# Batch 0's keys ahead of its values, and fences by halves, in a retention layer fused with a swish feed-forward

## Chip, cores and metric

The kernel runs on one core of one Trainium2 chip. The metric is the device time of one launch in microseconds (us). The kernel before took 292.37 us in the median of 3 runs (291.78 to 292.76).

An engine's short name is used throughout: PE is the matmul engine (PEld its weight loads), DVE the vector engine, ACT the scalar engine, POOL the engine that the code calls gpsimd, SP the engine whose queue issues nearly all DMAs (SPq in the profile).

## What is computed

A retention layer (attention with a decay instead of a softmax) for 8 batches, 8 heads, 576 positions and heads of 64, then a feed-forward layer with 2048 hidden units and the activation h * sigmoid(beta * h):

```python
scores = scale * np.matmul(q, k.transpose(0, 1, 3, 2))
gamma = 1.0 - 2.0 ** (-5.0 - np.arange(H))
Dmat = np.where(rel >= 0, gamma[:, None, None] ** rel[None, :, :], 0.0)   # rel = row - column
attn = np.matmul(scores * Dmat, v)
x = attn.transpose(0, 2, 1, 3).reshape(B * S, H * D)                      # 4608 x 512
h = x @ w_in                                                              # 512 x 2048
out = (h * (1.0 / (1.0 + np.exp(-beta * h)))) @ w_out                     # 2048 x 512
```

Inputs and output are float32; the matmuls run in bfloat16.

## The kernel before

**Tiling.** Each batch has 512 positions in four chunks of 128 (a pair of batch and chunk has one number, `i`; batch 0 has chunks 0 to 3) and a tail of 64; the eight tails make up a ninth block of 512 rows. The decay is put into q and v ahead of time (`gq`, `gv`), so that a causal mask is all that is left for the scores inside a chunk; what earlier chunks give comes through a running state, the 64 x 64 sum of k times v for each head. The output of a chunk is therefore masked scores times values (`a_O`, `outputs4`) plus queries times the state of all earlier chunks, the cross part (`a_cross`, `crosses4`).

**Batch 0** opens the kernel, with nothing beside it but loads and a few warm-up matmuls on zeros (`warm_up`, L259). For chunk `i`: `pre` (L324) casts the keys to bf16 on POOL (L354) and multiplies the values by their gain on POOL (L328); `t_k` transposes the keys on PE (L384) and copies them out on ACT (L385); `a_sc` makes the scores (L403, two PSUM banks, tag "sc" with 2 buffers, or "mm" for chunk 3) and DVE masks them (`R`, L407, two instructions); `a_st` (L464) adds this chunk to the state in PSUM (L472) and copies it as bf16 to `sbds[c]` (L478, two instructions of half the rows each on ACT); `a_cross` multiplies queries by `sbds[c - 1]` (L436); `a_O` multiplies masked scores by values (L450); `a_x` copies the output to `xT` (L459, L460, L462), the input of the up projection.

The order is written out by hand in the body of the kernel (from L856): all calls are recorded in that order, and each engine runs its own in that order. In PE's queue, batch 0's steps stand like this (sc scores, st state, x cross, O output, a number for the chunk): tk0 sc0 st0, tk1 O0 sc1 x1, tk2 st1 O1 sc2, tk3 sc3 x2 st2 O2, x3 O3, up projection with st3 in front of it.

**Loads.** SP issues q of batch 0, then keys and values in the order `ahead` (L108; a pair is chunk and 0 for keys or 1 for values), then the first weights in pieces (L185): three column pieces of 256, each as two halves of the rows, a fourth of 256 whole, then pieces of 512 columns by row halves. `cast_w_in` (L201) casts a piece to bf16: even row blocks on POOL (L206), odd ones on DVE (L208).

**The up projection of batch 0** follows the pieces: `ups` (L797) makes two or four column blocks of 128 for a half `u` of the rows, and then again for the other half; `up` makes one column block in one go (L714). `fill` (L910) is the list of these steps and, behind them, of all other up and down projections; `streams` holds all other work with a place in `fill`, to fractions of a step, at which `merged` puts it in.

**Batches 2 to 7** do all four chunks at once (`scores`, `outputs4`, `crosses4`, for the tails `tail_outputs`, `tail_crosses`). Here each matmul uses a quarter of the array: 64 rows (a half of the positions or one head of a pair) and 64 columns. A cross matmul (`cross`, L612) reads the rows `row_d(j)` and writes the output rows `row_d(j ^ y)`; `paired` deals the lists of `j = 0` and `j = 1` alternately onto PE. The outputs of half `x` are written by the row half `x` of the array; a cross with `j == x` may follow at once, one with `j != x` has to wait until the outputs in the same PSUM bank are done. For that there is `fence` (L504): a tiny ACT copy (L505) that waits for the last output matmul, and for which the first cross of the second kind on row half 0 waits. `crosses4` puts the state matmuls of the next batch between the two kinds (`ahead`) for batches 3 to 6. `both4` is outputs and crosses of one batch, put into `fill` at a place such as `t + 25.9`.

Of the kernel before, what the change touches and what calls it, by code (L numbers as in the profile page):

```python
# [14 lines left out]
ALU = mybir.AluOpType  # L15
# [4 lines left out]
def kernel(  # L20
# [86 lines left out]

    ahead = [(0, 0), (0, 1), (1, 0), (1, 1), (2, 0), (3, 0), (2, 1), (3, 1)]  # L108
    keys_first = [(0, 0), (1, 0), (0, 1), (1, 1), (2, 0), (3, 0), (2, 1), (3, 1)]
# [74 lines left out]
    low_rows, high_rows = slice(0, KO // 2), slice(KO // 2, KO)  # L184
    pieces = [(f, 256, (low_rows, high_rows) if f < 768 else (slice(0, KO),)) for f in range(0, d_ff // 2, 256)]  # L185
    pieces += [(f, 512, (w,)) for f in range(d_ff // 2, d_ff, 512) for w in (low_rows, high_rows)]
# [83 lines left out]
    def betas_safe():  # L270

        nc.gpsimd.tensor_tensor(tiny[:], beta_sb[:], beta_sb[:], ALU.mult)
        nc.gpsimd.tensor_scalar(tiny[:], tiny[:], 1e-24, 1e-12, ALU.is_lt, ALU.mult)
        nc.gpsimd.tensor_tensor(beta_sb[:], beta_sb[:], tiny[:], ALU.add)

# [20 lines left out]
    def gains(g, c):  # L296
        return g[:, c, :].unsqueeze(2).to_broadcast([P, H, D])
# [26 lines left out]
    def pre(i, js=(0, 1)):  # L324

        b, c = seq[i]
        if 0 not in js:
            nc.gpsimd.tensor_tensor(live[i]["vn"][:], kv_tiles.pop(i)[:, 1], gains(gv, row_of(b, c)), ALU.mult)  # L328
            return
# [134 lines left out]
    def a_st(i):  # L464

        b, c = seq[i]
        L = live[i]
        if c == 0:
            state_ps[b] = psum.tile([P, HP, P], F32, name="st", tag="st", bufs=1)
        st = state_ps[b]  # L470
        for p in range(HP):
            nc.tensor.matmul(st[:, p, :], heads(L["kn"], p), heads(L["vn"], p),  # L472
                             start=(c == 0 and p == 0), stop=True, skip_group_check=True)
        for j in range(2):
            r, cols = slice(j * D, (j + 1) * D), slice(j * D, (j + 1) * D)
            e = nc.vector.tensor_copy if i in (CB + 2, CB + 3) else nc.scalar.copy
            if c < CB - 1:
                e(sbds[c][r, :, cols], st[r, :, cols])  # L478
                continue
            e(ends[b][r, :2], st[r, :2, cols])  # L480
            e(ends[b][(1 - j) * D:(2 - j) * D, 2:], st[r, 2:, cols])
# [4 lines left out]
    def row_d(j):  # L486
        return slice(j * D, (j + 1) * D)
# [101 lines left out]
    def outputs4(b):  # L589

        i0 = b * CB
        O4, opened = new_O4(i0, [P, 2, CB, 2 * PC]), set()
        R = batch[b]["R"]
# [8 lines left out]
        for y in range(2):  # L602
            paired(*[[F(one, x, y, cc, pp, kind, hh ^ x) for cc in range(2) for pp in range(2) for kind in range(2)
                      for hh in range(2)] for x in range(2)])
        batch[b]["O4"] = O4, fence()

    def crosses4(b, later=None):
# [4 lines left out]
        def cross(j, e, y, pp, after):  # L612
            p, c, kind = 2 * y + pp, e // 2, e % 2
            w = c // 2 * PC + kind * PC // 2
            mm(O4[c % 2, y][row_d(j ^ y), pp, :, w:w + PC // 2], sbq[e - 1][row_d(j), p, :],
               q_cols(i0 + c, row_d(j), p, kind)[0], after=after)

        def crosses(j, x, after=None):
            return [F(cross, j, e, y, pp, after) for e in range(1, 2 * CB) if e // 2 % 2 == x for pp in range(2) for y in range(2)]

# [45 lines left out]
    def tail_outputs(i0):  # L666

        O4, opened, R = new_O4(i0, [P, 2, NT, TL]), set(), live[i0]["R"]

# [6 lines left out]
        for y in range(2):  # L676
            paired(*[[F(one, x, y, t, pp, hh ^ x) for t in range(NT) for pp in range(2) for hh in range(2)]
                     for x in range(2)])
        live[i0]["O4"] = O4, fence()

    def tail_crosses(i0, later):
# [3 lines left out]
        def cross(j, x, t, y, pp, after):  # L685
            p = 2 * y + pp
            mm(O4[x, y][row_d(j ^ y), pp, t, :], ends[2 * t + x][row_d(j), p, :], live[i0 + t]["qkT"][row_d(j), 0, p, half(x)],
               after=after)

        for own in range(2):  # L690
            paired(*[[F(cross, j, j ^ own, t, y, pp, after if own else None) for t in range(NT) for pp in range(2) for y in range(2)]
                     for j in range(2)])
# [164 lines left out]
    betas()  # L857
    betas_safe()
    for n in range(4):
        pre_q(0, n)  # L860
    t_q(0, 0)
    warm_up(1, 128)
    t_q(0, 1)
    pre(0)
    t_k(0)
    warm_up(2, 128)
    a_sc(0)
    a_st(0)
    pre(1)
    t_k(1)  # L870
# [4 lines left out]
    a_sc(1)  # L875
    a_cross(1, True)
    pre(2, (0,))
    t_k(2)
    a_st(1)
    a_O(1)  # L880
    pre(3, (0,))
    a_sc(2)
    t_k(3)
    a_x(1)
    warm_up(1, 128)
    a_sc(3)
    a_cross(2, True)
    pre(2, (1,))
    a_st(2)
    a_O(2)  # L890
    a_x(2)
    pre(3, (1,))
    warm_up(2, 128)
    a_cross(3, True)
    a_O(3)
    cast_w_in(0, (0, 1))
    a_x(3)
# [11 lines left out]

    fill = [F(ups, 0, (fo, fo + 1), u, tags) for fo, tags in ((0, ("mm", "mm")), (2, ("O", "O")), (4, ("sc", "sc"))) for u in range(2)]  # L910
    fill += [F(up, 0, fo) for fo in (6, 7)]
    for fo, tags in ((8, ("O", "O", "sc", "sc")), (12, ("mm", "mm", "mm", "st"))):
# [110 lines left out]
    for n in range(1, B):  # L1023
# [17 lines left out]
        elif n < SB:  # L1041
            streams.append([(t + 16, F(first_states, b))] * (b == XB + 1) +
                           [(t + 19, F(group1, b, (0, 1))), (t + 25.9, F(both4, b))])
        elif n == B - 1:
# [41 lines left out]
```

## Time and profile before

One execution was profiled: 292.13 us, of which its span (first to last instruction) is 290.4 us. PE's granted clock is 1.00 in every stage up to 270 us.

| engine | busy us | share of span | instructions |
|---|---|---|---|
| PE | 280.4 | 97% | 3357 |
| PEld | 171.3 | 59% | 3385 |
| ACT | 172.6 | 59% | 306 |
| DVE | 168.4 | 58% | 314 |
| POOL | 119.6 | 41% | 219 |

By stage, PE is busy for 14.95 us of the first 18 (with overlapping matmuls and warm-ups counted), 5.66 of the 6 up to 24 us, 8.95 of the 9 up to 33 us and 26.89 of the 27 up to 60 us. Batch 0's keys and values land from 7.4 to 15.8 us at about 220 GB/s, in the order of their issue, some 1.2 us apart: k0 7.43, v0 8.64, k1 9.9, v1 11.1 (both from when POOL takes them up), k2 12.25, k3 13.46, v2 14.66, v3 15.80. The halves of the first weight pieces follow at 16.56 and 17.35, and the fourth piece at 23.30.

The seven fences ran at 79.93, 109.14, 140.10, 161.06, 188.05, 217.03 and 245.34 us.

A timeline row is read like this: start in us, length in us, engine, line, operation, output<-inputs, shapes, how many are merged into the row, and in square brackets the idle time of the engine before it and what ended it. For a merged row the length runs from the first start to the last end. The chain of waits has start, length and what the time went to.

### The profile page before, as it was taken

To read this page: it belongs to the slowest core of one execution; us is meant where nothing else is said; L and a number is where in the kernel's file an instruction comes from. 1 tells how busy PE (TensorE), PEld (TensorE's weight loads), DVE (VectorE), ACT (ScalarE), POOL (GpSimd) and SP (SyncE) were. 2 spreads that over 40 slices of the span, in tenths; PEclk is the share of its full clock that TensorE was granted. 3 is DMA by queue.
4 is the path that set the end of the run, shared out by engine and by line. 5 is a ranking of instruction groups with operands and counts; after the bars stand their busy time and mean duration, and the time that the engine had idled before them with its cause. 6 is when DMAs were issued, how large, how long until landed. Compare 5 with 4: busy or idle time off the path is not lost.

```text
span 290.4 us, 8109 instructions
## 1 busy us (share of the span) xinstructions
PE 280.4 (97%) x3357; PEld 171.3 (59%) x3385; DVE 168.4 (58%) x314; ACT 172.6 (59%) x306; POOL 119.6 (41%) x219
## 2 busy tenths in 40 slices
PE   8899999999999999999999999999999999999995
PEld 6554446864544454445554885578557845784584
DVE  6563556804673375405538976986597555642673
ACT  4676646686639895882257725772576156837730
POOL 4765206782565473337349245615389000000000
PEclk9999999999999999999999999999999999999999
DMA  7999999999999999599999979996789130003004
GB/s 211 218 341 386 387 275 227 253 187 194 214 153 258 251 277 189 139 254 175 193 257 217 170 113 257 260 162 142 234 192 169 41 148 3 2 29 116 2 2 142
DMA packets 128884, 54.01 MB, mean 186 GB/s; under 512 B 110400, under 2 KB 121680, under 8 KB 128848
## 3 DMA queue, kind: packets, MB, share of 16 engines
q1 hardware_dynamic: 128816, 53.49, 82.9%
q8 instruction: 26, 0.43, 0.7%
q14 instruction: 10, 0.08, 0.1%
q10 hardware_dynamic: 32, 0.01, 0.0%
HBM read 36.71 MB, written 9.44 MB: 159 GB/s over the span
## 4 chain that ended last, share of the span: by engine, by line
PE 86%; SPq 6%; DMA 4%; issue 1%; DVE 1%; POOL 1%; ACT 0%; DVEq 0%; POOLq 0%
PE ph L714 39%; PE po L824 16%; PE U L751 9%; PE Z L751 6%; PE W L751 6%; SPq L100 3%; PE O L499 3%; DMA wt<-in_moe_w_in_dram 3%; PE ph L806 2%; DMA kvn<-in_k_dram 2%; PE sc L499 1%; PE st L499 1%; SPq L198 1%; PE sc L403 0%; DVE sum L535 0%
## 5 line engine op out<-in xcount | busy, mean ns | idle before, releaser
L714 PE MATMUL ph<-xT,w_in_sb 128*128 128x512 bf16 (+1 forms) x544 | 113.9, 363 | 1.4 <-issue 0.6
L721 ACT ACTIVATE gT<-ph,beta_sb 128x512 bf16<-128x512 f32 (+1 forms) x100 | 63.6, 644 | 42.1 <-PE ph L714 41.2
L714 PEld LDWEIGHTS <-w_in_sb 128*128 128x128 bf16 x560 | 53.5, 98 | 55.7 <-POOL w_in_sb L206 0.9
L824 PE MATMUL po<-w_out_sb,gT 128*128 128x512 bf16 x246 | 56.2, 379 | 1.2 <-issue 1.0
L354 POOL CAST kn<-kvn 128x128 bf16<-128x128 f32 (+2 forms) x80 | 30.2, 411 | 58.1 <-DMA kvn<-in_k_dram 57.7
L751 PEld LDWEIGHTS <-sa 128*128 128x128 bf16 x400 | 39.2, 98 | 4.5
L719 DVE TENSOR_SCALAR gT<-hs,ratio 128x512 bf16<-128x512 f32 x40 | 23.8, 594 | 29.1 <-ACT hs L718 28.9
L824 PEld LDWEIGHTS <-gT 128*128 128x128 bf16 x256 | 24.2, 98 | 27.8
L317 POOL TENSOR_TENSOR qs<-qn,gq 128x256 bf16<-128x256 f32 (+1 forms) x36 | 27.5, 792 | 23.3 <-DMA qn<-in_q_dram 14.8
L328 POOL TENSOR_TENSOR vn<-kvn,gv 128x512 bf16<-128x512 f32 x32 | 34.4, 1079 | 4.9 <-DMA kvn<-in_v_dram 4.4
L718 ACT ACTIVATE hs<-ph,beta_sb 128x512 f32<-128x512 f32 x40 | 27.5, 687 | 14.4 <-PE ph L714 13.8
L735 DVE TENSOR_TENSOR sa<-gT 128x1024 bf16<-128x1024 bf16 (+1 forms) x45 | 33.9, 792 | 1.1 <-PE Z L751 0.9
L286 DVE TENSOR_TENSOR R<-sc,late 128x512 bf16<-128x512 f32 x24 | 15.3, 680 | 22.3 <-PE sc L499 12.1
L751 PE MATMUL Z<-b,sa 128*128 128x256 bf16 x160 | 19.1, 273 | 0.0
L751 PE MATMUL U<-b,sa 128*128 128x256 bf16 x160 | 19.1, 273 | 0.0
L248 DVE TENSOR_TENSOR b<-wt 128x512 bf16<-128x512 f32 x20 | 13.8, 736 | 7.1 <-ACT b L244 7.1
L751 PEld LDWEIGHTS <-gT 128*128 128x128 bf16 x160 | 15.6, 98 | 2.9
L407 DVE TENSOR_TENSOR R<-sc,causal 128x512 bf16<-128x512 f32 x16 | 10.2, 686 | 4.6 <-PE sc L403 4.5
L806 PE MATMUL ph<-xT,w_in_sb 128*128 128x512 bf16 x54 | 12.3, 379 | 0.3 <-ACT xT L460 0.2
L809 ACT ACTIVATE gT<-ph,beta_sb 128x512 bf16<-128x512 f32 x14 | 8.6, 686 | 4.2 <-PE ph L806 4.2
L831 ACT COPY ot<-po 128x512 f32<-128x512 f32 x12 | 7.0, 583 | 6.8 <-PE po L824 6.7
L629 ACT CAST xT<-O 128x512 bf16<-128x512 f32 x17 | 8.8, 597 | 2.5 <-PE O L499 2.5
(117 smaller groups left out, 294.4 us busy)
## 6 DMA issues: line engine op xcount, KB each, us to landing
qn<-in_q_dram SPq DMA_DIRECT2D x16, 512.0 KB, 5.4
out_dram<-ot SPq DMA_DIRECT2D x32, 256.0 KB, 3.3
kvn<-in_k_dram SPq DMA_DIRECT2D x20, 256.0 KB, 5.8
kvn<-in_v_dram SPq DMA_DIRECT2D x20, 256.0 KB, 5.6
wt<-in_moe_w_out_dram SPq DMA_DIRECT2D x8, 512.0 KB, 9.0
kvn<-in_k_dram SPq DMA_DIRECT2D x24, 128.0 KB, 4.1
kvn<-in_v_dram SPq DMA_DIRECT2D x24, 128.0 KB, 3.7
wt<-in_moe_w_in_dram SPq DMA_DIRECT2D x5, 512.0 KB, 8.7
```

Of the source, the lines that this page charges most:

```text
L286: return lambda: f(*a)
L317: nc.gpsimd.tensor_tensor(batch[b]["qs"][:, cs, to], q_tiles[b][:, hs, cs].rearrange("p h i d -> p i h d"), gq[:, cs, hs].unsqueeze(3).to_ ...
L328: nc.gpsimd.tensor_tensor(live[i]["vn"][:], kv_tiles.pop(i)[:, 1], gains(gv, row_of(b, c)), ALU.mult)
L354: nc.gpsimd.tensor_copy(kn[:, c % 2, to], t[:, 0, hs])
L714: nc.tensor.matmul(ph, w_in_sb[:, ko, fo * P:(fo + 1) * P], xts[m][:, ko, :, w], start=(ko == 0), stop=(ko == KO - 1))
L718: nc.scalar.activation(h, ph, ACT.Silu, scale=beta_sb[:, fo:fo + 1])
L719: nc.vector.tensor_scalar(gts[m][:, fo], h, ratio[:, fo // 2:fo // 2 + 1], None, ALU.mult)
L721: nc.scalar.activation(gts[m][:, fo, :, w], ph, ACT.Silu, scale=beta_sb[:, fo:fo + 1])
L735: nc.vector.tensor_tensor(sums_a[0][:, held_in[j], ks], quarter(m, *x, ks), quarter(m, *y, ks), op)
L751: nc.tensor.matmul(chains[c, n][:, 0 if alone else p], a, sevens[k // 2][:, j - 1, k % 2, :], start=j in (3, 4, 1) and k == 0 and (alone o ...
L806: nc.tensor.matmul(phs[f][:], w_in_sb[:, ko, f * P:(f + 1) * P], xts[m][:, ko], start=(ko == 0), stop=(ko == KO - 1))
L824: nc.tensor.matmul(po[:, :nn], gT[:, fo, ms, :], w_out_sb[:, fo, n0:n0 + nn], start=(fo == 0), stop=(fo == FO - 1))
```

## The change

- `ahead`: keys of chunks 1, 2 and 3 are loaded before the values of chunk 1.
- The fourth weight piece is loaded by halves of its rows like the first three, and its up projection (column blocks 6 and 7) goes by halves, with `ups`.
- `betas_safe` (three small instructions on a 128x16 tile) moves from POOL to DVE, and behind the queries' transposes.
- In PE's queue, batch 0 now stands: tk0 sc0 st0, tk1 O0 sc1, tk2 sc2, tk3 sc3, x1 st1 O1, x2 st2 O2, x3 O3, up projection, with one more small warm-up behind tk2.
- The values of chunk 3 are multiplied half by POOL and half by DVE, and of the state copy after chunk 2 the second half goes to DVE.
- Outputs are fenced in two halves (`y = 0`, `y = 1`), the crosses of `crosses4` and `tail_crosses` are sorted by `y`, and the first cross of each half waits for its own fence.
- `both4` of batch 3 comes one step of `fill` later.

```diff
-    ahead = [(0, 0), (0, 1), (1, 0), (1, 1), (2, 0), (3, 0), (2, 1), (3, 1)]
+    ahead = [(0, 0), (0, 1), (1, 0), (2, 0), (3, 0), (1, 1), (2, 1), (3, 1)]
...
-    pieces = [(f, 256, (low_rows, high_rows) if f < 768 else (slice(0, KO),)) for f in range(0, d_ff // 2, 256)]
+    pieces = [(f, 256, (low_rows, high_rows)) for f in range(0, d_ff // 2, 256)]
...
     def betas_safe():
 
-        nc.gpsimd.tensor_tensor(tiny[:], beta_sb[:], beta_sb[:], ALU.mult)
-        nc.gpsimd.tensor_scalar(tiny[:], tiny[:], 1e-24, 1e-12, ALU.is_lt, ALU.mult)
-        nc.gpsimd.tensor_tensor(beta_sb[:], beta_sb[:], tiny[:], ALU.add)
+        nc.vector.tensor_tensor(tiny[:], beta_sb[:], beta_sb[:], ALU.mult)
+        nc.vector.tensor_scalar(tiny[:], tiny[:], 1e-24, 1e-12, ALU.is_lt, ALU.mult)
+        nc.vector.tensor_tensor(beta_sb[:], beta_sb[:], tiny[:], ALU.add)
...
         if 0 not in js:
-            nc.gpsimd.tensor_tensor(live[i]["vn"][:], kv_tiles.pop(i)[:, 1], gains(gv, row_of(b, c)), ALU.mult)
+            v, g = kv_tiles.pop(i)[:, 1], gains(gv, row_of(b, c))
+            if i == CB - 1:
+                for e, hs in ((nc.gpsimd, slice(0, HP)), (nc.vector, slice(HP, H))):
+                    e.tensor_tensor(live[i]["vn"][:, hs], v[:, hs], g[:, hs], ALU.mult)
+            else:
+                nc.gpsimd.tensor_tensor(live[i]["vn"][:], v, g, ALU.mult)
             return
...
-            e = nc.vector.tensor_copy if i in (CB + 2, CB + 3) else nc.scalar.copy
+            e = nc.vector.tensor_copy if i in (CB + 2, CB + 3) or i == CB - 2 and j else nc.scalar.copy
...
         for y in range(2):
             paired(*[[F(one, x, y, cc, pp, kind, hh ^ x) for cc in range(2) for pp in range(2) for kind in range(2)
                       for hh in range(2)] for x in range(2)])
-        batch[b]["O4"] = O4, fence()
+            fences.append(fence())
+        batch[b]["O4"] = O4, fences
...
-               q_cols(i0 + c, row_d(j), p, kind)[0], after=after)
+               q_cols(i0 + c, row_d(j), p, kind)[0], after=after and after[y])
...
-            return [F(cross, j, e, y, pp, after) for e in range(1, 2 * CB) if e // 2 % 2 == x for pp in range(2) for y in range(2)]
+            return [F(cross, j, e, y, pp, after) for y in range(2) for e in range(1, 2 * CB) if e // 2 % 2 == x for pp in range(2)]
...
-            paired(*[[F(cross, j, j ^ own, t, y, pp, after if own else None) for t in range(NT) for pp in range(2) for y in range(2)]
+            paired(*[[F(cross, j, j ^ own, t, y, pp, after if own else None) for y in range(2) for t in range(NT) for pp in range(2)]
                      for j in range(2)])
...
     t_q(0, 1)
+    betas_safe()
     pre(0)
...
-    pre(1)
+    pre(1, (0,))
     t_k(1)
     warm_up(1, 128)
     a_cross(0, True)
     a_O(0)
     a_x(0)
     a_sc(1)
-    a_cross(1, True)
     pre(2, (0,))
     t_k(2)
+    warm_up(1, 128)
+    a_sc(2)
+    pre(3, (0,))
+    t_k(3)
+    warm_up(1, 128)
+    a_sc(3)
+    pre(1, (1,))
+    a_cross(1, True)
     a_st(1)
     a_O(1)
-    pre(3, (0,))
-    a_sc(2)
-    t_k(3)
     a_x(1)
-    warm_up(1, 128)
-    a_sc(3)
+    pre(2, (1,))
     a_cross(2, True)
-    pre(2, (1,))
     a_st(2)
     a_O(2)
+    pre(3, (1,))
     a_x(2)
-    pre(3, (1,))
     warm_up(2, 128)
     a_cross(3, True)
+    cast_w_in(0, (0, 1))
     a_O(3)
-    cast_w_in(0, (0, 1))
     a_x(3)
...
-    fill = [F(ups, 0, (fo, fo + 1), u, tags) for fo, tags in ((0, ("mm", "mm")), (2, ("O", "O")), (4, ("sc", "sc"))) for u in range(2)]
-    fill += [F(up, 0, fo) for fo in (6, 7)]
+    fill = [F(ups, 0, (fo, fo + 1), u, tags) for fo, tags in ((0, ("mm", "mm")), (2, ("O", "O")), (4, ("sc", "sc")), (6, ("mm", "st"))) for u in range(2)]
...
-                           [(t + 19, F(group1, b, (0, 1))), (t + 25.9, F(both4, b))])
+                           [(t + 19, F(group1, b, (0, 1))), (t + (26.7 if n == 2 else 25.9), F(both4, b))])
```

`tail_outputs` and the waiting cross of `tail_crosses` change in the same way as `outputs4` and `cross`.

More of the change, by code (lines that the diff above doesn't have):

```diff
@@ L591, in outputs4 @@
         i0 = b * CB
-        O4, opened = new_O4(i0, [P, 2, CB, 2 * PC]), set()
+        O4, opened, fences = new_O4(i0, [P, 2, CB, 2 * PC]), set(), []
         R = batch[b]["R"]
@@ L666, in tail_outputs @@
     def tail_outputs(i0):
-        O4, opened, R = new_O4(i0, [P, 2, NT, TL]), set(), live[i0]["R"]
+        O4, opened, R, fences = new_O4(i0, [P, 2, NT, TL]), set(), live[i0]["R"], []
         def one(x, y, t, pp, hh):
@@ L678, in tail_outputs @@
                      for x in range(2)])
-        live[i0]["O4"] = O4, fence()
+            fences.append(fence())
+        live[i0]["O4"] = O4, fences
     def tail_crosses(i0, later):
@@ L687, in cross @@
             mm(O4[x, y][row_d(j ^ y), pp, t, :], ends[2 * t + x][row_d(j), p, :], live[i0 + t]["qkT"][row_d(j), 0, p, half(x)],
-               after=after)
+               after=after and after[y])
         for own in range(2):
-            paired(*[[F(cross, j, j ^ own, t, y, pp, after if own else None) for t in range(NT) for pp in range(2) for y in range(2)]
+            paired(*[[F(cross, j, j ^ own, t, y, pp, after if own else None) for y in range(2) for t in range(NT) for pp in range(2)]
                      for j in range(2)])
@@ L857 @@
     betas()
-    betas_safe()
     for n in range(4):
```

## The prediction

> **What bounds the kernel now.** I read the page first: PE is busy for 280.4 of 290.4 us, and the chain that ended last is 86% PE. So a stage can only give what PE waits in it. Next I read that chain in order of time, for the point from which PE waits for nothing outside itself.
>
> ```profile
> PE 86%; SPq 6%; DMA 4%; issue 1%; DVE 1%; POOL 1%; ACT 0%; DVEq 0%; POOLq 0%
> ...
> 15.74 7.56 DMA wt<-in_moe_w_in_dram
> 23.30 0.05 issue
> 23.36 0.53 POOL w_in_sb L206
> 23.89 0.05 issue
> 23.93 1.90 PE ph L714 x8
> 25.83 4.32 PE ph L806 x20
> ```
>
> Columns are start, length, what. The fourth piece of the first weights lands at 23.30, POOL casts it, PE takes it at 23.93. Afterwards the chain is PE without a break. Everything before 24 us is thus a race between weights that land and batch 0's attention, which has to be finished before any up projection (L806) can start. The timeline shows both sides:
>
> ```profile
> 12.33 1.29 DVE L407 TENSOR_TENSOR R<-sc,causal 128x512 bf16<-128x512 f32 x2 [0.82 <-PE sc L403]
> ...
> 13.89 0.76 ACT L478 CAST sbd<-st 64x256 bf16<-64x256 f32 x2
> 14.04 0.40 PE L403 MATMUL sc<-qT,kT 64*128 64x128 bf16 x8
> ...
> 14.73 2.18 POOL L328 TENSOR_TENSOR vn<-kvn,gv 128x512 bf16<-128x512 f32 x2 [0.60 <-DMA kvn<-in_v_dram]
> ...
> 16.43 0.74 ACT L478 CAST sbd<-st 64x256 bf16<-64x256 f32 x2 [0.55 <-PE st L472]
> ...
> 17.23 0.40 PE L436 MATMUL O<-qT,sbd 128*128 128x128 bf16 x4
> 17.56 0.41 PE L450 MATMUL O<-R,vn 128*64 128x128 bf16 x8
> ...
> 18.48 5.34 PE L806 MATMUL ph<-xT,w_in_sb 128*128 128x512 bf16 x23 [0.17 <-ACT xT L460]
> ...
> 25.63 6.62 PEld L806 LDWEIGHTS <-w_in_sb 128*128 128x128 bf16 x32 [0.29 <-POOL w_in_sb L206]
> 25.67 7.07 PE L806 MATMUL ph<-xT,w_in_sb 128*128 128x512 bf16 x31
> ```
>
> Batch 0's first up projection runs from 18.48. It is 64 matmuls of 0.216 us (1.73 us for 8), 13.8 us, and ends at 25.67 + 32 x 0.216 = 32.58: PE waits only 0.28 us in it, for the fourth piece. Even the next piece is just in time (the PEld row at 25.63 waits for POOL's cast).
>
> Last I read the timeline around the fences (ACT L505). I call the stretch from the first cross (O<-qT,sbd or O<-kT,end) to the next 128-row matmul the cross block.
>
> ```profile
> 108.44 1.04 POOL L328 TENSOR_TENSOR vn<-kvn,gv 128x512 bf16<-128x512 f32 x1
> ...
> 109.14 0.20 ACT L505 COPY fenced<-lscale 128x2 f32<-128x2 f32 x1
> 109.53 0.19 PE L499 MATMUL st<-vn,kn 64*64 64x64 bf16 x1 [0.44 <-POOL vn L328]
> ...
> 160.21 0.71 PE L499 MATMUL O<-R,vn 64*64 64x64 bf16 x64
> ...
> 217.27 0.10 PEld L499 LDWEIGHTS <-sbd 64*64 64x64 bf16 x1 [0.22 <-ACT fenced L505]
> ```
>
> Three blocks stand still at the fence: 0.33 us at 79.9, 0.30 at 217.0, 0.22 at 245.4. Batch 3's stands for 0.63 us at 108.9, for batch 4's values on POOL. In the other three (140, 161, 188) the states of the next batch fill the wait.
>
> **The opening.** Loads: same bytes, other order. The landings are 1.2 us apart, so k2 comes at 11.05 instead of 12.25, k3 at 12.25 instead of 13.46, v1 at 13.46 instead of 11.05; v2 (14.66), v3 (15.80) and all weights stay. The extra weight DMA is one more issue of about 0.47 us on SP, which issues a weight piece 8 us before it lands (16.25 to 24.65): nothing. If that lead were gone, it would cost its 0.47.
>
> The safe betas leave POOL (6.39 to 8.02 there), so k0, landed at 7.43, is cast 0.5 us earlier. On DVE they are three 128x16 instructions, by the two like them (L901 0.24, L902 0.17) 0.5 to 0.7 us; DVE is idle from 8.76 to 10.21, which hides them; without that, the first mask is later by as much.
>
> Now the path. Chunk 1 is freed as before by k1 (cast from 9.9): its scores come at 11.6, behind the output of chunk 0 on PE, its masks (1.29) from 12.1 to 13.4. The scores of chunk 2 need the two "sc" banks that these masks read, so they start at 13.46. Before, the cross, state and output of chunk 1 stood ahead of them on PE; now PE goes on with t_k(3) at 13.77, ACT copies it (0.43 after, 0.58 long) until 14.79, and scores 3 come at 14.85. All of chunk 1's state work is queued behind that: cross 15.16, state 15.39, though its values are ready at 14.55 (13.46 + 1.04 on POOL). Then the serial chain runs: states to bf16 on ACT (0.43 after, 0.76) 15.82 to 16.58; cross 2 16.64, state 2 16.86; its copy, now shared by ACT and DVE (half of 0.76), 17.29 to 17.67; the warm-up of 0.5 us that stands ahead of cross 3 begins at about 17.5 and lets it go at 18.1; output 3 at 18.43; the copy to xT (0.5 after, 0.43) to 19.35. The first up projection starts at 19.4. In the old order the same steps with the same durations reproduce 18.5, where the trace has 18.48.
>
> What else is shared: the last values, POOL half (half of 1.04) done at 16.4, DVE half (128x256, half of a 0.69 product) queued behind DVE's state copy until 18.0, ahead of output 3 at 18.43: nothing. It would be next if the state chain were 0.4 us quicker.
>
> Start 0.93 later; but all weights are then cast when PE asks (the fourth piece at 23.9, needed at 24.6), so the 0.28 us of waiting vanish: 19.4 + 13.82 = 33.23 against 32.58, **+0.65 us**. So the fourth piece by halves is worth nothing by itself: even with a start in time, PE would only stand at the cast of the next piece (25.6) instead. Bounds: -0.05 (start not later than 18.5) to +1.0 (start 19.75, for the 0.3 us by which such steps can add up). I take +0.65. Downstream nothing absorbs it, as PE waits for no other engine by more than 0.2 us from 26 to 68 us, and the second weights land by 39.6, ahead of their use after 40.4.
>
> **The fences.** One more ACT copy of 0.19 us each, 7 in all; ACT is 59% busy and PE waits for it in three blocks only. Batch 3's block moves one step (4 matmuls, 0.86 us) later, past POOL's 109.48: its 0.63 us go.
>
> But crosses are now sorted by y, and that decides where on the array they run. A cross reads rows j and writes columns j^y. Before, y alternated: four 64x64 tiles in turn. Now y=0 gives only tiles (0,0) and (1,1), y=1 only (0,1) and (1,0). The 64 outputs at 160.21, four tiles in turn, take 0.71 us with 0.19 for the last: 8 ns each, 32 ns until the same tile is used again. No two-tile row of 64 columns exists; with 128 columns, the eight matmuls at 17.56 in two column tiles take (0.41 - 0.22)/7 = 27 ns each, 54 for a pair, as long as one untiled matmul of 128 columns (56). So a tile isn't quicker when fewer are in use, and a pair of crosses will take 27 (half of 54) to 32 ns instead of 16. I take 32, the row of the same size.
>
> The Trainium skill, "TensorEngine Tiling (Array Packing)", Key Properties, says that different tiles work in parallel, which speaks against this order, and the trace agrees where four tiles are in use (8 ns each at 160.21). "TensorE: Matmul & The Clock Gate", Back-to-back issue gap, gives N/2.4 + 2.5 ns, 29 ns for 64 columns (an estimate from that page of the Trainium skill; the pair of 128 columns at 17.56 agrees, 54 ns against its 56); by it the blocks would cost about +0.2 us in sum.
>
> Blocks now (cross to next 128-row matmul): 1.18, 1.76, 1.48, 1.21, 1.34, 1.15, and 1.10 for the tails, 9.22 us in sum. After: batches 2 and 7 have 28 two-tile pairs, 0.85 us to the last start; batch 2's fence is then covered, batch 7's first half fence still comes after ACT's activation (216.92 + 0.19, PE at 217.22), so 0.95. Batches 3 to 6 have 32 two-tile pairs and 12 four-tile ones, about 1.14 us. Tails: 32 pairs in two halves, 0.97. With the closing 0.36 us (80.43 to 80.78) each: 1.2, four times 1.5, 1.3, 1.33, in sum 9.83: **+0.6 us**, the won 0.63 included. Bounds: with 27 ns -0.2; upwards +0.25 more, if batches 4 and 6 keep steps of 60 to 115 ns that stand in their blocks now and are drowned in my count.
>
> **Sum.** +0.65 + 0.6 = +1.25 us. The profiled execution took 292.13 us (span 290.4, 1.73 around it): 293.4. It lies 0.24 under the median; from the median I get 293.6. I say 293.5.
>
> **Rivals.**
> (1) The opening's delay is hidden, the crosses still slow down: for it, PE has waits of up to 0.6 us between 8 and 18 us (0.60 before L384 at 8.64, 0.40 before L403 at 15.45), which a re-ordered PE may use; against it, the chain above already runs through them. 292.25 + 0.6 = 292.9 (292.25 is the middle of median and profiled run).
> (2) The order of the crosses is free: tiles are held by issue and not by streaming. For it, in steady stretches crosses follow each 8.3 ns as if paced by issue (24 at 160.73 in 0.43 - 0.19 us). Then batch 3's 0.63 and 0.13 of batch 2's stall are won and the tails lose 0.05 to the second fence, -0.7, against +0.65 in the opening: 292.2, no change.
> (3) Faster: the waits at the crosses. Their place is the four standing blocks; the price is -0.7 us with free order. It decides as soon as the first up projection starts by about 18.8, where the landing weights hide the rest of a late start: 292.25 - 0.7 - 0.05 = 291.5. Against it, the banks and the single PE queue that I traced above.
> That the change does not do what it says is partly in my forecast: the fourth piece by halves removes a wait that a late start has already removed.
>
> **How the numbers follow.** Forecast 0.66, own range 292.7 to 294.3; rival 1 0.12; rival 2 0.08; rival 3 0.14. About 0.3% (0.9 us) is what a measurement of this kernel tells from no change, so slower means over 293.25 and faster under 291.5. Slower: 0.58 of the forecast and 0.02 of rival 1, 0.60. Same: 0.08 of the forecast, 0.10 of rival 1, rival 2, 0.04 of rival 3, 0.30. Faster: 0.10 of rival 3. The range 292.2 to 294.3 leaves out rival 3 and 0.04 above: it holds the late opening with 27 ns pairs (+0.45) and the upper bounds of both (+1.0 and +0.85).
>
> **What would show it.** The first L806 matmul near 19.4 and no PE wait near 23.9; scores of chunk 3 before the state of chunk 1 on PE; first down projection near 33.2. In the cross blocks, pairs 32 ns apart, blocks of batches 4 to 6 at about 1.5 us, the tails' at 1.33, no wait on vn in batch 3's. Wrong if L806 starts before 18.9, or if two-tile crosses still come 8 ns apart.

## The result, and the profile after

The changed kernel took 293.85 us in the median of 7 runs (293.07 to 294.42), the kernel before 292.50 in 7 runs beside them (291.74 to 292.95): a ratio of 1.0048 with a 95% interval of 1.0029 to 1.0067, slower by 0.8 to 2.0 us. The profiled execution took 293.85 us with a span of 292.13, which is 1.73 over the span of before. Lines of code that follow are those of the changed kernel, 5 to 7 higher than before (first scores L408, masks L412, state L477, quarter-array matmuls L504, first up projection L813, first down projection L831), except where a run is the kernel before with an edit.

I laid the two traces beside each other by the ends of ACT's instructions, which are the same in both but for the fences. The changed kernel is 1.38 us late at the first down projection; it loses 0.15 more at batch 2's cross block, gains 0.29 at batch 3's and 0.11 near 138 us, loses 0.37 at batch 5's, 0.02 at batch 7's and 0.13 at the tails. That is 1.65 of the 1.73; the last 0.08 come behind ACT's last instruction.

The opening first. These are rows of the timeline after (start, length, engine, line, operation, what ended the idle time before it):

```profile
9.10 1.04 POOL L333 TENSOR_TENSOR vn<-kvn,gv 128x512 bf16<-128x512 f32 x1 [0.69 <-DMA kvn<-in_v_dram]
9.19 0.98 DVE L273 TENSOR_SCALAR tiny<-tiny 128x16 f32<-128x16 f32 x1
...
10.19 0.61 POOL L359 CAST kn<-kvn 128x512 bf16<-128x512 f32 x1
...
10.20 0.63 DVE L274 TENSOR_TENSOR beta_sb<-beta_sb,tiny 128x16 f32<-128x16 f32 x1
...
10.75 1.28 DVE L412 TENSOR_TENSOR R<-sc,causal 128x512 bf16<-128x512 f32 x2
...
11.39 0.59 ACT L390 COPY kT<-T 128x512 bf16<-128x512 bf16 x1
...
12.08 0.38 PE L455 MATMUL O<-R,vn 128*64 128x128 bf16 x7 [0.38 <-DVE R L412]
...
12.40 0.40 PE L408 MATMUL sc<-qT,kT 64*128 64x128 bf16 x8
...
15.56 0.40 PE L408 MATMUL sc<-qT,kT 64*128 64x128 bf16 x8 [0.40 <-ACT kT L390]
...
16.12 0.39 PE L477 MATMUL st<-vn,kn 128*128 128x128 bf16 x4
...
18.02 0.37 ACT L483 CAST sbd<-st 64x256 bf16<-64x256 f32 x1
...
18.42 0.43 DVE L483 CAST sbd<-st 64x256 bf16<-64x256 f32 x1 [1.14 <-ACT sbd L483]
```

Scores of chunk 3 (15.56) stand ahead of the state of chunk 1 (16.12), as I traced it. What I had not foreseen is in the upper rows: the second betas instruction takes 0.98 us and the third 0.63, though the first of the same size took 0.17 (at 8.99). Both end within 0.04 us of POOL's instruction beside them (10.14 and 10.80). The first mask starts at 10.75, though the scores, begun at 9.53, were done at 9.93. The output of chunk 0 waits for the masks until 12.08. The scores of chunk 1 stand behind it on PE and start at 12.40, though their transposed keys were copied by 11.98. The last two rows are the state copy that ACT and DVE now share: DVE's half begins only when ACT's half is done.

The chain of waits after has the first projections, and much later it goes through POOL's products for batch 6, which it did not before (start, length, what):

```profile
20.15 13.97 PE ph L813 x64
34.12 10.36 PE po L831 x48
...
153.63 3.75 POOL qs L317 x5
...
159.69 1.25 POOL kn L359 x2
160.94 1.45 POOL vn L333
162.39 0.04 issue
162.43 0.19 PE st L504
```

PE runs the 64 matmuls of the first up projection without a break, 20.15 to 34.12: the wait of 0.28 us near 23.9 is gone, and the start is 1.67 later than before. In batch 5's cross block the state matmuls of batch 6 wait until POOL's last values are done at 162.39.

The third view is the timeline of the tails' cross block after. The first eight crosses of kT belong to y=0, as do the eight of qT that PE's program has next; the second eight of kT belong to y=1 and come behind those in the program.

```profile
246.62 0.32 PE L504 MATMUL O<-kT,end 64*64 64x64 bf16 x8
246.76 0.20 PE L504 MATMUL O<-qT,end 64*64 64x64 bf16 x2
246.78 0.22 PE L504 MATMUL O<-kT,end 64*64 64x64 bf16 x2
246.79 0.22 PE L504 MATMUL O<-qT,end 64*64 64x64 bf16 x3
```

The kT row at 246.78 begins after two of y=0's eight qT: matmuls of the other two tiles overtake the ones that still wait for their own. By the single starts, a tile is used again after 31 to 32 ns, as I took it; but with overtaking the 64 crosses start within 0.87 us (246.616 to 247.482), 27 ns a pair.

The next table has the same measure for every block, from the start of its first cross to that of its last, in us (b2 is batch 2); the rows below that of after are experiments that are told further on. It leaves out the closing step to the next 128-row matmul. That step showed 0.35 before and 0.125 after, because the trace of before lacks the first matmul behind the blocks: after, the second matmul comes 0.226 us behind the first, and 0.125 and 0.226 make the 0.35.

| kernel | b2 | b3 | b4 | b5 | b6 | b7 | tails | sum |
|---|---|---|---|---|---|---|---|---|
| before | 0.83 | 1.40 | 1.11 | 0.83 | 0.97 | 0.79 | 0.74 | 6.67 |
| after | 1.00 | 0.98 | 1.13 | 1.22 | 0.98 | 0.84 | 0.87 | 7.02 |
| before, crosses by y | 0.97 | 1.14 | 1.13 | 0.97 | 0.97 | 0.92 | 0.89 | 6.99 |
| before, two blocks later | 0.83 | 0.83 | 0.97 | 0.84 | 0.91 | 0.79 | 0.74 | 5.91 |
| after, three edits | 0.89 | 0.98 | 1.05 | 0.99 | 0.99 | 0.86 | 0.86 | 6.62 |
| the same, one fence | 0.83 | 0.86 | 0.97 | 0.84 | 0.97 | 0.87 | 0.75 | 6.09 |

### The profile page after: what moved, and what is told of

Same layout as the page of the kernel before. It is cut to its first block, busy times and chain, and to the rows that moved or that the text cites. A ratio compares the mean times of both kernels' runs of the same rounds, so it can differ in the third digit from the quotient of the medians.

```text
span 292.1 us, 8156 instructions
## 1 busy us (share of the span) xinstructions
PE 283.9 (97%) x3387; PEld 172.7 (59%) x3387; DVE 168.5 (58%) x319; ACT 173.6 (59%) x312; POOL 119.5 (41%) x216
## 4 chain that ended last, share of the span: by engine, by line
PE 78%; DMA 10%; POOL 5%; DVE 2%; SPq 1%; issue 1%; ACT 1%; POOLq 0%; ACTq 0%
PE ph L721 29%; PE po L831 14%; PE U L758 9%; PE Z L758 6%; PE W L758 6%; DMA qn<-in_q_dram 5%; PE ph L813 5%; PE O L504 3%; POOL qs L317 2%; DMA kvn<-in_k_dram 2%; POOL kn L359 1%; DMA kvn<-in_v_dram 1%; POOL vn L333 1%; PE sc L504 1%; DMA out_dram<-ot 1%
## 5 line engine op out<-in xcount | busy, mean ns | idle before, releaser
L728 ACT ACTIVATE gT<-ph,beta_sb 128x512 bf16<-128x512 f32 (+1 forms) x98 | 62.4, 645 | 41.7 <-PE ph L721 41.0
L721 PEld LDWEIGHTS <-w_in_sb 128*128 128x128 bf16 x552 | 53.0, 98 | 54.2 <-issue 0.2
L831 PE MATMUL po<-w_out_sb,gT 128*128 128x512 bf16 x256 | 57.8, 379 | 0.0
L831 PEld LDWEIGHTS <-gT 128*128 128x128 bf16 x256 | 24.2, 98 | 27.8
L726 DVE TENSOR_SCALAR gT<-hs,ratio 128x512 bf16<-128x512 f32 x40 | 21.3, 532 | 30.6 <-ACT hs L725 30.5
L333 POOL TENSOR_TENSOR vn<-kvn,gv 128x512 bf16<-128x512 f32 x31 | 35.0, 1139 | 3.9 <-DMA kvn<-in_v_dram 3.6
L813 PE MATMUL ph<-xT,w_in_sb 128*128 128x512 bf16 x64 | 14.0, 379 | 0.2 <-ACT xT L465 0.2
L816 ACT ACTIVATE gT<-ph,beta_sb 128x512 bf16<-128x512 f32 x16 | 9.9, 687 | 4.3 <-PE ph L813 4.3
L412 DVE TENSOR_TENSOR R<-sc,causal 128x512 bf16<-128x512 f32 x16 | 10.2, 685 | 2.8 <-PE sc L408 2.6
L813 PEld LDWEIGHTS <-w_in_sb 128*128 128x128 bf16 x64 | 6.2, 98 | 7.6 <-POOL w_in_sb L206 0.3
```

The source lines that it names most:

```text
L333: nc.gpsimd.tensor_tensor(live[i]["vn"][:], v, g, ALU.mult)
L721: nc.tensor.matmul(ph, w_in_sb[:, ko, fo * P:(fo + 1) * P], xts[m][:, ko, :, w], start=(ko == 0), stop=(ko == KO - 1))
L726: nc.vector.tensor_scalar(gts[m][:, fo], h, ratio[:, fo // 2:fo // 2 + 1], None, ALU.mult)
L728: nc.scalar.activation(gts[m][:, fo, :, w], ph, ACT.Silu, scale=beta_sb[:, fo:fo + 1])
L813: nc.tensor.matmul(phs[f][:], w_in_sb[:, ko, f * P:(f + 1) * P], xts[m][:, ko], start=(ko == 0), stop=(ko == KO - 1))
L831: nc.tensor.matmul(po[:, :nn], gT[:, fo, ms, :], w_out_sb[:, fo, n0:n0 + nn], start=(fo == 0), stop=(fo == FO - 1))
```

## Experiments

Each kernel ran 12 times (betas on POOL: 5) beside 29 to 35 runs of the kernel before on the same chip; the first row is the result above, 7 runs beside 7. The runs form three groups, each on a chip of its own, and the kernel before differs between them (292.64 to 292.77), so the ratios are what to compare. The four below the first row take the change apart. Diffs are shown in part, cut at three dots.

| run | median us | ratio to before | 95% interval |
|---|---|---|---|
| after | 293.85 | 1.0048 | 1.0029 to 1.0067 |
| betas on POOL | 293.58 | 1.0037 | 1.0024 to 1.0050 |
| opening alone | 293.45 | 1.0022 | 1.0009 to 1.0036 |
| fences alone | 292.82 | 1.0020 | 0.9997 to 1.0042 |
| shift alone | 292.25 | 0.9986 | 0.9972 to 1.0000 |
| state first | 293.00 | 1.0011 | 0.9996 to 1.0025 |
| betas late | 293.88 | 1.0053 | 1.0029 to 1.0076 |
| crosses by y | 293.12 | 1.0016 | 1.0002 to 1.0031 |
| two shifts | 291.64 | 0.9966 | 0.9951 to 0.9981 |
| after, b5 later | 293.32 | 1.0016 | 0.9996 to 1.0036 |
| three edits | 293.07 | 0.9997 | 0.9978 to 1.0017 |
| three edits, one fence | 292.29 | 0.9981 | 0.9960 to 1.0003 |
| fences, b5 later | 292.60 | 0.9990 | 0.9968 to 1.0011 |

**Opening alone**: the changed kernel with fences, crosses and batch 3's place as before.

```diff
...
-            fences.append(fence())
-        batch[b]["O4"] = O4, fences
+        batch[b]["O4"] = O4, fence()
...
-                           [(t + 19, F(group1, b, (0, 1))), (t + (26.7 if n == 2 else 25.9), F(both4, b))])
+                           [(t + 19, F(group1, b, (0, 1))), (t + 25.9, F(both4, b))])
```

> The changed kernel with the old fences, the old order of the crosses and the old place of batch 3's block: the opening alone. Theory 1 (the opening costs 1.4 us, as the trace of the changed kernel has it): +1.4 us over the kernel before, up projections end near 34.0. The prediction's size: +0.65 us, end near 33.2.

**Fences alone**: the kernel before with all edits at the cross blocks, the opening as before.

> The kernel before with fences by halves, crosses sorted by y and batch 3's block one step later: the fences alone. By the trace of the changed kernel +0.3 us, of which batch 3 gives -0.3, batch 2 +0.15, batch 5 up to +0.35, tails +0.15. The prediction's size (two tiles at 32 ns a pair in strict order): +0.6. Rival, order free: -0.7.

In time the two parts are worth +0.22% and +0.20%, together what the whole change costs. In the trace of the opening alone the first up projection starts at 19.51 and the first down projection at 33.32, 0.74 late. In the trace of the fences alone the gain at batch 3 (0.4 to 0.6 us) is given back at batch 5's block (0.6 us), and 0.2 more goes at batch 6's and at the tails.

**Betas on POOL**: the changed kernel with the three betas instructions on POOL, at their new place.

```diff
-        nc.vector.tensor_tensor(tiny[:], beta_sb[:], beta_sb[:], ALU.mult)
+        nc.gpsimd.tensor_tensor(tiny[:], beta_sb[:], beta_sb[:], ALU.mult)
...
```

> The changed kernel with the three instructions of betas_safe on POOL again, at their new place. Theory 1 (on DVE they wait for POOL's key cast and value product, so that the mask of chunk 0 starts at 10.75 us instead of 10.1): mask 0 near 10.1, first up projection at 19.4 to 19.6 us instead of 20.15, total 0.6 us under the changed kernel, +0.7 over the one before. Theory 2 (the new order of PE's queue alone makes the start late): first up projection stays at 20.0 to 20.2, total as the changed kernel.

The first mask starts at 9.78, the first up projection at 19.33 and the first down projection at 33.14 (0.56 late). That is 0.8 us ahead of the whole change, but the betas are less than half of it. From the start of POOL's first value product to the scores of chunk 1 it is 2.94 us here (8.65 to 11.59). It is also 2.94 in the opening alone (8.83 to 11.77), although there the second betas instruction took 1.00 us on DVE and the first mask came at 10.03. In the change it is 3.30 (9.10 to 12.40). So of the 0.8 us, 0.45 is that the first values landed later in that execution, and 0.36 is what the held betas cost there; in the opening alone they cost the path nothing. In total time the two can't be told apart (1.0037 and 1.0048).

Two more readings point to POOL's instruction as what holds DVE up. In the changed kernel with batch 5 later POOL's product began at 9.21, behind the first two betas instructions; all three took 0.17 us, and the scores of chunk 1 came 2.93 us after the product, at 12.14. And the third instruction was held only in the change, where it began 10 ns behind POOL's cast; in the opening alone and with the state first the two begin within 1 ns of each other, and it took 0.17 and 0.18 us.

**Betas late**: still on DVE, but moved to just ahead of the reciprocal behind batch 0's chunks.

```diff
     t_q(0, 1)
-    betas_safe()
...
+    betas_safe()
     nc.vector.reciprocal(rbeta_sb[:], beta_sb[:])
```

> The changed kernel with the three betas instructions still on DVE, but moved from before batch 0 to just ahead of the reciprocal that follows batch 0's chunks. Theory (DVE's small instructions end only when POOL's product or cast ends, and that delays the masks): masks 0 start when the scores are done, at 9.8 instead of 10.75, the first up projection at 19.2 to 19.5 instead of 20.15, the first down projection near 33.2; total like that with the betas on POOL, 293.2 to 293.6, or 0.1 to 0.3 less as POOL is freed of them too. Rival (the wait on DVE is no part of the path; the queue order alone makes the late start): first up projection at 19.9 or later, total 293.8.

The trace has the starts that the theory says: masks at 9.72, up projection at 19.43, down projection at 33.25. But the first values were early too: POOL's first product began at 8.76, and the scores of chunk 1 came 2.94 us behind it, as with the betas held in the opening alone. The time missed its 293.2 to 293.6: 293.88. The execution profiled lost part of it again at batch 5's block (0.53 us of waiting for the values of batch 6, which landed late), so the total says nothing on the betas.

**State first**: chunk 1's cross and state ahead of chunk 3's scores, one warm-up less.

```diff
     t_k(3)
-    warm_up(1, 128)
-    a_sc(3)
     pre(1, (1,))
     a_cross(1, True)
     a_st(1)
+    a_sc(3)
     a_O(1)
```

> The changed kernel with chunk 3's key transposes, chunk 1's cross and chunk 1's state work put ahead of chunk 3's scores on PE again (one warm-up less there); everything else as changed, betas on DVE still beside POOL. Theory 1 (the delay of the opening is the queue order on PE: state 1 stood behind scores 3): state 1 starts near its values' readiness, about 15 us instead of 16.12, and the first up projection at 18.9 to 19.4 instead of 20.15; total 0.6 to 1.0 under the changed kernel, 292.9 to 293.2. Theory 2 (the delay is the late masks, because the betas on DVE wait for POOL's products, and order only shuffles it): masks 0 still near 10.7, the first up projection stays at 19.8 or later, total 293.5 or more.

Rows of its timeline, in the same columns:

```profile
14.67 0.38 PE L477 MATMUL st<-vn,kn 128*128 128x128 bf16 x4 [0.19 <-POOL vn L333]
14.99 0.40 PE L408 MATMUL sc<-qT,kT 64*128 64x128 bf16 x8
```

The state of chunk 1 now starts when its values are ready, 14.67, and the first up projection starts at 18.68, the first down projection at 32.49 (32.58 before). The second betas instruction took 0.99 us on DVE there too and put the first mask at 10.04. The dropped warm-up can't be the reason: in the change PE waits another 0.40 us behind it, for ACT's copy of the keys. So the late opening is the order in PE's queue; what the betas add in the change comes on top. In time it is the change with one edit, 1.0011 against 1.0048, 1.1 us less, and the two intervals don't overlap. The execution profiled (293.42) lost 1.06 us at batch 5's block, so there the early start isn't all in the time.

**Shift alone**: the kernel before with batch 3's block one step later. This run and those down to the three edits are about the waits for POOL.

```diff
-                           [(t + 19, F(group1, b, (0, 1))), (t + 25.9, F(both4, b))])
+                           [(t + 19, F(group1, b, (0, 1))), (t + (26.7 if n == 2 else 25.9), F(both4, b))])
```

> The kernel before with batch 3's block one step later and nothing else. If batch 3's wait of 0.63 us for POOL's values is won in full and nothing waits later: -0.6 us. If the wait moves (to batch 5's values, or is given back at the next scores): -0.3 us or less.

In its trace, one of the quickest of its executions (291.40), PE is 0.71 us ahead from 116 us on and stays so to the end; in time 0.14% (0.4 us, from 0 to 0.8) are left.

**Two shifts**: batch 5's block one step later as well.

```diff
-            by = t + 14.5 if n == SB else t + 12.8
+            by = t + 15.5 if n == SB else t + 12.8
```

> The kernel before with batch 3's block one step later and batch 5's block one step later too. Theory (the 0.6 us won at batch 3's block is given back at batch 5's where POOL's values for the next batch come late; with that block later they can't be late): PE runs 0.6 to 0.7 us ahead from 116 us on and keeps it to the end, total 291.6 to 291.9, and the scatter of the runs is smaller than with one shift alone. Rival (what was won is given back elsewhere, for instance by the tails or the last weights, whichever block is moved): 292.2 to 292.5. If moving batch 5's block starves what follows it, slower than before.

291.64 us, 0.9966 of before: the one kernel here that is surely faster. Against the shift alone (0.9986) it isn't sure, as the intervals overlap, and the runs scatter hardly less (1.7 us against 1.9). Its trace fell 0.4 us behind at 75 us, in a wait that the shift alone did not have, won 0.56 at batch 3's block and kept it; at the end it is 0.25 ahead. Its values for batch 6 are done at 159.55, its first state matmul comes at 161.71 and waits for nothing:

```profile
158.52 1.03 POOL L328 TENSOR_TENSOR vn<-kvn,gv 128x512 bf16<-128x512 f32 x1
...
161.71 0.19 PE L499 MATMUL st<-vn,kn 64*64 64x64 bf16 x1
```

**Why POOL's values come late at batch 5.** Without the second shift, six of the seven executions whose opening or whose batch 3 was changed waited there (0.25 us after, 0.30 betas on POOL, 1.00 opening alone, 0.48 fences alone, 1.06 state first, 0.53 betas late; the shift alone did not); with it one of five did (0.34 us). These are steps from one matmul's start to the next; the idle time in the profile's brackets counts from an end and is some 0.2 less. The timeline of the opening alone, beside that of before, shows how the values get late:

```profile
159.18 1.98 POOL L359 CAST kn<-kvn 128x256 bf16<-128x256 f32 x3
159.44 1.57 DVE L740 TENSOR_TENSOR sa<-gT 128x1024 bf16<-128x1024 bf16 x2
...
161.13 1.21 POOL L333 TENSOR_TENSOR vn<-kvn,gv 128x512 bf16<-128x512 f32 x1
...
162.39 0.19 PE L504 MATMUL st<-vn,kn 64*64 64x64 bf16 x1 [0.81 <-POOL vn L333]
```

```profile
157.69 1.06 POOL L354 CAST kn<-kvn 128x256 bf16<-128x256 f32 x3
...
158.72 1.04 POOL L328 TENSOR_TENSOR vn<-kvn,gv 128x512 bf16<-128x512 f32 x1
...
159.96 0.68 DVE L735 TENSOR_TENSOR sa<-gT 128x1024 bf16<-128x1024 bf16 x1
```

Before, POOL is done (159.76) when DVE's two long products `sa` begin at 159.96. In the opening alone they begin at 159.44, in the middle of POOL's key casts, which then take 1.98 us instead of 1.06. That the products hold POOL up is read from such pairs, no run tried it. In the betas late run, and in the changed kernel with batch 5 later, POOL's casts were not held, and the values' DMA itself landed later (POOL idle for 1.8 to 2.0 us before its last product).

**After, b5 later**: the changed kernel with the same edit at batch 5.

> The changed kernel with one edit: batch 5's cross block one step later (its due time t + 15.5 instead of t + 14.5). Theory (what is won at batch 3's block is given back at batch 5's, where PE waits for POOL's values of batch 6): no wait for the values product at 162 any more, 0.3 to 0.9 under the changed kernel, 293.0 to 293.6. Rival (batch 5's wait is a small part, and the loss is the opening and the fences alone): 293.7 to 293.9.

293.32, inside the expected range; no wait for values at batch 5. The ratio fell from 1.0048 to 1.0016 (the intervals overlap), though in this one execution the trace gives only 0.2 us of it to that block and 0.27 to an opening that ran quicker.

**Three edits**: chunk 1's state first, betas on POOL, batch 5's block later.

> The changed kernel with three edits: chunk 1's state ahead of chunk 3's scores, betas on POOL, batch 5's block one step later. Theory (opening's loss is queue order and betas; the third loss is batch 5's wait; only the fences' cost of 0.2 to 0.5 is left, against 0.6 to 0.7 won at batch 3): first up projection at 18.0 to 18.6, first down projection at 31.9 to 32.5, total 291.7 to 292.3. Rival (something else in the change costs): 292.6 or more.

**Three edits, one fence**: the same with crosses in the old order and one fence.

> As the run with three edits, but with the crosses in the old order and one fence for both halves as before. Theory (the sorted crosses with fences by halves cost 0.2 to 0.5): 0.2 to 0.5 less than that run, 291.3 to 291.8, at or under the kernel before with the two shifts (291.64). Rival (the halves of the fence pay for the order): equal to that run or slower.

**Fences, b5 later**: the kernel before with all edits at the cross blocks and batch 5's block later.

> The kernel before with all of the change's edits at the cross blocks (fences by halves, crosses sorted by y, batch 3's block later) and batch 5's block one step later too. Differs from the kernel before with the two shifts (291.64) by fences and order alone. Theory (tiles overtake, so a part of the cost of two-tile crosses is left): 0.2 to 0.5 over it, 291.85 to 292.15. Strict order as predicted: 1.0 or more over it, 292.6 or more. Free: 291.5 to 291.7.

**Crosses by y**: the kernel before with only the order of the crosses changed.

```diff
-            return [F(cross, j, e, y, pp, after) for e in range(1, 2 * CB) if e // 2 % 2 == x for pp in range(2) for y in range(2)]
+            return [F(cross, j, e, y, pp, after) for y in range(2) for e in range(1, 2 * CB) if e // 2 % 2 == x for pp in range(2)]
...
```

> The kernel before with one edit: the crosses sorted by y, still with one fence for both halves. Theory of the prediction (PE takes them in strict order, 32 ns for a pair in two tiles): blocks of four-tile batches grow by 0.3 to 0.4 us each, in sum +1.0 to +1.4 with the won fence waits left out, total 293.3 to 293.7. Theory 2 (matmuls of other tiles overtake, so that two pairs run beside each other after a short time): +0.1 to +0.5, total 292.4 to 292.8. Theory 3 (the order is free): 292.3, no change.

The four go together. The order alone costs 0.16% (0.46 us, from 0.06 to 0.9): what was expected of overtaking tiles (0.1 to 0.5), and less than the 1.0 to 1.4 of strict order. Pairs of kernels that differ by fences and order alone differ by 0.16% (three edits, with and without), 0.24% (two shifts) and 0.34% (shift alone against fences alone): 0.5 to 1.0 us. The two intervals of each pair overlap, so no pair shows it by itself; the three agree in sign. The table of blocks gives the same: 6.62 in sum with three edits (6.72 for the change with batch 5 later) against 6.09 with one fence, 5.91 with two shifts and 6.18 with the shift alone. So half a fence doesn't pay for the order that it needs.

The run with three edits missed its 291.7 to 292.3 (293.07, no change against before). In its trace PE waited for POOL's casts of later weight pieces, 0.35 us until 27.80 and 0.14 until 29.68, and so lost the early start (18.74) until the first down projection at 33.14; 0.18 more went at 41. That with one fence had no such wait (32.45) and came to 292.29, above the two shifts and above its 291.3 to 291.8. The fences with batch 5 later missed their 291.85 to 292.15. They came to 292.60, the number that strict order would give, but not by its way: the blocks at batches 2, 3, 7 and the tails are as long as in the other kernels with this order (0.89, 0.98, 0.86 and 0.86; batch 4's 1.23 is longer, without a single long wait), and the execution profiled waited 0.34 us at batch 5's block and 0.59 of idle time at batch 6's, for values that POOL made behind a key cast of 1.98 us:

```profile
185.90 1.98 POOL L354 CAST kn<-kvn 128x256 bf16<-128x256 f32 x3
...
189.11 0.19 PE L499 MATMUL st<-vn,kn 64*64 64x64 bf16 x1 [0.59 <-POOL vn L328]
```

## Why the prediction came out as it did

The time (293.5 predicted, 293.85 measured) and the sign were right, and the opening was right in its mechanism. That the sum is so near is in part luck: two errors in the cross blocks cancel.

**Opening, +0.65 us.** The step held: scores 3 ahead of state 1 delay the serial chain, and undoing just that (state first) took the delay away. From the scores of chunk 1 to the first up projection the five executions with this order need 7.73 to 7.75 us, where I had 7.8 (11.6 to 19.4); the three with the state first need 6.90 to 7.01. The five reach the first down projection at 33.14, 33.25, 33.32, 33.69 and 33.96, where I said 33.2; the whole opening costs 0.22% (0.65 us, from 0.3 to 1.05) in time. What differs between the five lies ahead of the scores of chunk 1 (11.59, 11.70, 11.77, 12.14 and 12.40, where I said 11.6). It is how late the first values reach POOL and, in the change alone, the betas. The profiled execution of the change is the latest of the five.

The step that failed in it is "DVE is idle from 8.76 to 10.21, which hides them": I costed the betas at 0.5 to 0.7 us by two instructions of DVE that had nothing of POOL's beside them, and here they last as long as POOL's product and cast, until 10.83. They put the first mask 0.8 us behind its scores. That cost 0.36 us of the start in the execution of the change, and nothing in the opening alone and with the state first, where only the second of them was held. The Trainium skill, "SBUF — State Buffer", Who interferes with whom, says that some DVE instructions contend with POOL for a shared port pair, and that whoever issues first has the pair for its whole instruction while the other is blocked. The trace agrees, with 0.98 and 0.63 us that end with POOL's instruction.

A second step was wrong and did not show. I had the state copy shared by ACT and DVE done in half of 0.76 us; the halves run one behind the other, 18.02 to 18.85, and so in all eight kernels that have it (what makes DVE wait for ACT was not tried). Cross 3 starts 0.05 us behind it, at 18.90, 1.30 us after state 2. I had 1.24, because I let a warm-up hold cross 3 back, so the sum came out right by luck there.

**Fourth weight piece by halves, nothing.** The wait of 0.28 us is gone, as said, under a later start. Where the start was early the down projection came 0.09 us (state first, 18.68) and 0.13 us (three edits, one fence, 18.64) earlier than before: so much it is worth there. In another execution (three edits) PE stood 0.35 us for a later piece. I had put that next stand at 25.6; it ended at 27.80, one piece on.

**Fences, +0.6 us.** Two terms were wrong. "I take 32" ns for each pair, in strict order, was right for the tile and wrong for the queue: I had 0.85 us from first to last cross for batch 2, 0.95 for batch 7, 1.14 for each of batches 3 to 6 and 0.97 for the tails, 7.3 in sum; the changed order without a wait has 6.6 to 6.7. Against the old order without a wait (5.9 to 6.2) it costs 0.4 to 0.8 us instead of the 1.24 that I had put in before the won wait. The Trainium skill, "TensorE: Matmul & The Clock Gate", The mechanism, says that matmuls start strictly in the program's order; the starts of this trace differ (kT at 246.78 before most of qT), and the measurement decides. The other term, "batch 3's 0.63 us go", held where it stood (no wait on values at 111 after) but not to the end: PE came to batch 5's block earlier or in another phase, and waited for POOL's values there. I had looked at POOL's 1.3 us of slack at 161 for none of the edits. The closing 0.36 us of each block, which I had in both of my sums, holds a matmul that the trace lacks; it cancels. Net, after has 0.35 us more in its blocks than before, 0.25 of it that new wait; in time the fences alone cost 0.20% (0.6 us, from -0.1 to 1.2).

**Rivals.** A hidden opening (292.9) fell by the down projection 0.56 us late or more in every execution with this order. Free order (292.2) fell by the crosses by y; the 24 crosses that I gave for it take 10 ns each by their row (0.24 us), not 8.3. The faster rival's point, a first up projection by 18.8, was reached with the state first, and no kernel with the sorted crosses was measurably faster than before: its -0.7 at the blocks isn't there. The kernel that is faster (two shifts) has the old order.

**What stays open.** Executions of one kernel differ by 1 to 4 us in most of these runs, and the traces put part of it to waits that come and go: values at batches 5 and 6, the weight piece at 27. Whether DVE's products or the values' DMA start it in an execution was not tried, nor why the first values land at 8.58 us in one execution and at 9.06 in another.

## What to carry to other kernels

Before an early start or a won wait is booked to the end, follow the engine that feeds the next two joins: here POOL's values had 1.3 us of slack at batch 5, and six of seven kernels with a changed phase spent it; with that join moved by one step as well, a change at the edge of the noise (0.14%) became a clear one (0.34%). An instruction moved to an idle engine is costed by a row with the same neighbour on the other engine beside it, not by the fastest row of its size; whether the loss reaches the end is then read from the next join. A serial chain at the opening is shortened by what stands first in its queue, so put the work that the chain waits for ahead of work that only has to be done some time.

## What the hardware showed that I had not expected

A DVE instruction on 128x16 float32 took 0.17 us alone and 0.98 to 1.00 beside POOL's product of 128x512, ending with it. One that began 10 ns behind POOL's cast lasted 0.63 us, and those within 1 ns of it 0.17 and 0.18; the same stretch goes the other way, POOL's three key casts 1.98 us instead of 1.06 beside DVE's products. Quarter-array matmuls of free tiles start before earlier ones of the program that wait for theirs: 27 ns a pair where strict order would give 32. And a trace can lack the same matmul in every block of one execution and have it in another, which looks like a gap of 0.35 us that a change took away.
